# Two FNet and attention layers on one core: three roundings put off, one subtraction moved to VectorE, a bank held longer, the layer norm two steps later

## The chip, the cores and the metric

The kernel runs on one core of a Trainium2 chip. A core has five engines that work side by side, each through its own instructions in the order in which the program issues them: TensorE (PE in the profile; its weight loads are listed apart, as PEld), VectorE (DVE), ScalarE (ACT), GpSimd (POOL) and SyncE (SP, which here only starts DMAs). They wait for each other through semaphores. PE writes its products into PSUM, which has eight banks of 128 x 512 f32; ACT and DVE read PSUM, POOL works only on tiles in SBUF. The metric is the device time of one execution in microseconds, the median of several.

## The reference

Four sublayers work on x (2048 tokens by 512, f32), with a residual sum around each:

```python
x = x + fourier(layernorm(x))
x = x + attention(layernorm(x))
x = x + fourier(layernorm(x))
x = x + attention(layernorm(x))
```

`fourier` is the real part of a DFT over the hidden dimension and over the tokens, given as matrices: with a = x Wd_re and b = x Wd_im it is y = Ws_re a - Ws_im b. `attention` has 32 query heads of 16 and one key and value head shared by all; softmax(q k / 4) v, then the output matrix wo. All of it is f32, so the kernel splits every f32 operand of a product into a high part rounded to the fast product type (fp32r) and a low part, the difference, and multiplies high by high, high by low and low by high (`mm3`).

## The kernel before

The work is split into 16 tiles of 128 tokens (NT) and the sequence DFT into four groups of 512 output tokens (`tb`, 0 to 3). Each of the two layers has a phase A (Fourier, with keys, values and queries of the attention) and a phase B (attention, with the layer norm of the next layer).

**Phase A.** For each group `tb` the sum over the 16 token tiles is made first for the real matrix (c = 0), then for the imaginary one (c = 1). So there are 128 steps n = 32 tb + 16 c + s, with s the token tile. A step multiplies the tile's normalised x (`xnh`, `xnl`) with a piece of the DFT matrix (`ch`, `cl`), into the four banks of tag "x": z[0] to z[3], one for each 128 of the hidden dimension. From n = 48 on (`ROWS`) two steps are done together by `z_rows`, on two halves of PE's rows: in quarters q = 0 to 3 of such a pair the one half of the array works on one bank and the other half on another; banks 0 and 1 are written in quarter 0 and 2, banks 2 and 3 in 1 and 3. After quarters 0 and 1 stands a `relay`, an ACT copy of one column of `xnl` onto itself, which keeps the two halves in order. At the end of a chunk (s = 15) `z_split` copies the banks to SBUF rows on ACT (line 857, "raw"), rounds each to its high part on ACT (line 79) and subtracts for the low part on POOL (line 80). The raw copy is what sets a bank free for the next chunk.

The results of one group are then multiplied with the hidden DFT (`y_tile`, `y_rows`), added to x, and prepared for the attention in the next group's steps (`prep_tasks`, whose work stands in `inner[n, d]`, after quarter-step d of step n): layer norm, four transposes into bank z (`tr_tile`, line 275, with the copies of `split_act` on ACT, lines 83 and 84, and its subtraction on POOL, line 85), keys and values (`kv`, lines 88 to 90), their transposition (`v_tr`, lines 339 and 340, in bank z too) and the queries (`q_mm`).

**Early maxima.** Softmax needs the largest score of each row. Part of these scores is computed already in phase A, in the gaps of DVE and ACT: the table `EARLY` lists groups of score products with a first step and a due step. `pump` is called between PE's products and puts out one product (line 526) if a planner, a Python model of the clocks of PE, DVE and ACT (`clk`, advanced by `spend`), says that a bank is free: the one of tag "z" or one of the three of tag "y". There are three kinds: a whole product whose maximum DVE takes directly (part "u", line 542), a difference product whose positive part ACT writes to SBUF (part "d", line 530, Relu), and a base product that DVE adds to such a part while taking the maximum (part "b", line 536). `flush(n)` forces out what is due at step n. `held` tells the planner until when a bank is taken. All of this is fixed when the program is built; on the chip the engines only follow the order.

**Phase B.** For each of 16 query tiles i there are 32 steps of four score products (line 1086, tag "x"), four exponentials on ACT (line 1088) and the products with v (line 1100); in between the remaining maxima of the next tile (lines 435 and 1046 on PE, 436 and 1051 on DVE, with a one-element DVE copy, 1048, that keeps an order). At step 25 POOL rounds the negated maxima of the next query tile (`max_neg_b`, lines 588 and 589), at step 26 DVE transposes them (`max_rows`, line 594) and DMAs from SP's and POOL's queues put them beside the queries. `out_tasks(i)` lists what becomes of the tile before: its output product, and in the first layer the next layer norm: `o_ln` (line 191 on POOL), `o_xnh` (1250) and `o_xnl` (1254), at steps 25, 26 and 27. In a step the tasks of `out_tasks` are issued ahead of those of `half_tasks` and of `max_neg_b` and `max_rows`. In the last layer the three norm tasks issue nothing.

Of the kernel before, what the change touches and what calls it, by code (L numbers as in the profile page):

```python
# [22 lines left out]
NT = S // P  # L23
# [25 lines left out]
def fnet_mqa_kernel(ctx: ExitStack, tc: tile.TileContext, x_in, ct, dt_, wq, wkv, wo, out):  # L49
    nc = tc.nc  # L50
# [5 lines left out]
    def f(ap):  # L56
        return ap.bitcast(F32)
# [21 lines left out]
        nc.scalar.copy(hi, raw)  # L79
        (eng or nc.vector).tensor_sub(lo, raw, f(hi))  # L80

    def split_act(ps_, hi, lo, raw, neg=False):
        nc.scalar.activation(raw, ps_, AF.Copy, scale=-1.0 if neg else 1.0)
        nc.scalar.copy(hi, raw)
        nc.gpsimd.tensor_sub(lo, raw, f(hi))

    def mm3(ps_, ah, al, bh, bl, start, stop):
        nc.tensor.matmul(ps_, ah, bh, start=start, stop=False)  # L88
# [108 lines left out]
    def make_layer(L, src, mid, dst, last):  # L197
# [69 lines left out]
        def wq_load(g):  # L267
            wq_get(g, [half(2 * (g % 2) + j, F32R) for j in range(2)])

        def tr_tile(t, x, xth, xtl, raw=None):  # L270
            spend(pe=0.6, act=1.2)
            clk["z"] = clk["act"]
            pt = bank("z")
            for k in range(NK):
                nc.tensor.transpose(pt[:, k * P:(k + 1) * P], x[:, k * P:(k + 1) * P], ident)
            v = [ap.rearrange("p (a b) -> p a b", a=NK) for ap in (pt, raw or pt)]
            if raw:
                split_act(v[0], xth, xtl, v[1])
            else:
                split_ps(v[0], xth, xtl)  # L280

# [54 lines left out]
        def v_tr(t0, n, vt):  # L336
            pv_ = bank("z")[:, :n * 32].rearrange("p (t d) -> p t d", t=n)
            for j in range(n):
                nc.tensor.transpose(pv_[:, j, :], vt[32:64, j * P:(j + 1) * P], ident[32:64, 32:64])
            nc.scalar.copy(v1[:, t0:t0 + n, :DH], pv_[:, :, DH:])  # L340

        def q_mm(tb, g, xth, xtl):
            wh, wl = st["wqh", g]
# [157 lines left out]
        def issue(e, pr, g, force):  # L501
            i, kb = EARLY[e][:2]
            tag = "z" if clk["z"] <= clk["y"][0] and not st["hold"] else "y"
            free = clk["z"] if tag == "z" else clk["y"][0]
            part = "u"
            if len(kb) == 2:
                t = turn(e, g)
                if t is None:
                    return False
                part, pr, m = t  # L510
            if part == "b":
                free = max(free, st["rel"][e, pr, g][2] - 0.7)
            if free > clk["pe"] + 0.05 and not force:
                return False
            if tag == "y" and st.get("kept") == 1:
                return False
            if "mxe" not in st:
                st["mxe"] = sb.tile([P, len(KEPT), NPAIR, 2], F32, name="mxe")
            to = st["mxe"][:, KEPT.index(EARLY[e]), pr, g:g + 1] if i else partial(0)[:, pr, g, kb[0]:kb[0] + 1]
            gs = slice(64 * g, 64 * g + KR)  # L520
            k, c0 = (st["kd"], 0) if part == "d" else (kz, 512 * kb[-1])
            pm = bank(tag)
            if tag == "y" and st.get("kept"):
                st["kept"] -= 1
                assert st["kept"]
            nc.tensor.matmul(pm, o.qT[i][gs, pr, :], k[gs, c0:c0 + 512], start=True, stop=True)  # L526
            ready = max(clk["pe"], free) + 0.5
            if part == "d":
                r = sb.tile([P, 512], F32, name=m)
                nc.scalar.activation(r, pm, AF.Relu)  # L530
                end = serve("act", max(ready, clk.get(m, 0.0)))
                st["rel"][e, pr, g] = r, m, end
                seen[e][0][g] += 1
            elif part == "b":
                r, m, done = st["rel"].pop((e, pr, g))
                nc.vector.tensor_tensor_reduce(r, pm, r, 1.0, -3.0e38, ALU.add, ALU.max, to)
                end = clk[m] = serve("dve", max(ready, done))
                seen[e][1][g] += 1
                if i == 0 and (pr, g) == (NPAIR - 1, 1):
                    nc.gpsimd.tensor_copy(partial(0)[:, :, :, kb[1]], partial(0)[:, :, :, kb[0]])  # L540
            else:
                nc.vector.reduce_max(to, pm, axis=AX.X)
                end = serve("dve", ready)
            held(tag, end)
            clk["pe"] += 0.116
            return True
# [188 lines left out]
        def prep_tasks(tb, x1):  # L735
            base = 32 * (tb + 1)
            ts = {}

            def alloc():
                st["xt"] = [slot(2 + j, F32R).rearrange("p (k t) -> p k t", k=NK) for j in range(2)]  # L740

            def tr(tt):
                xth, xtl = st["xt"]
                cs = slice(tt * P, (tt + 1) * P)
                tr_tile(4 * tb + tt, x1[tt], xth[:, :, cs], xtl[:, :, cs], half(4 + tt))

            def do_kv():
                st["vt"] = kv(4 * tb, 4, *st["xt"], now=False)

            def ap(j):  # L750
                return lambda: (spend(dve=0.8), ln_apply(x1[j], x1[j], 4 * tb + j))

            def hold():
                st["hold"] = True

            def tr_(tt):
                st["hold"] = False
                tr(tt)

            def root_(e):  # L760
                roots[e] = ln_root(4 * tb + e, 2)

            ts[0, 0] = [alloc, lambda: root_(0)]
            ts[0, 2] = [lambda: ln_inv(*roots[0])]
            ts[1, 1] = [ap(0), lambda: root_(2)]
            ts[1, 2] = [ap(1), hold]
            ts[1, 3] = [lambda: ln_inv(*roots[2])]
            ts[2, 0] = [vacate, lambda: tr_(0)] + ([k_raw] if tb == 2 else [])
            ts[2, 1] = [hold]
            ts[2, 2] = [ap(2)]  # L770
            ts[2, 3] = [ap(3), lambda: tr_(1)]
            ts[3, 0] = [hold]
            ts[3, 1] = [lambda: tr_(2)]
            ts[3, 2] = [hold]
            ts[4, 0] = [lambda: tr_(3), lambda: [wq_load(g) for g in range(2)]]
            ts[4, 3] = [lambda: keep(2.6)]
            ts[5, 1] = [do_kv]
            ts[6, 0] = [lambda: (kv_lo(4 * tb, 4), k_diff(tb)), hold]
            ts[6, 2] = [lambda: (st.update(hold=False), v_tr(4 * tb, 4, st["vt"]))]
            for g in range(4):  # L780
                ts[6 + g, 1] = [lambda: keep(0.9)]
                ts[6 + g] = [lambda g=g: q_mm(tb, g, *st["xt"])]
                if g < 2:
                    ts[6 + g].append(lambda g=g: wq_load(g + 2))
                if g:
                    ts[6 + g].append(lambda g=g: q_store(tb, g - 1))
            ts[10] = [lambda: q_store(tb, 3)]
            return {(base + k[0], k[1]) if isinstance(k, tuple) else base + k: v for k, v in ts.items()}

        def phase_a(extra):  # L790
# [53 lines left out]
                ks = iter(range(1, 9))  # L844
                return lambda: at.get(next(ks), lambda: None)()

            def z_split(z, hi, lo, c, d, row):
                if d % 2 == 0:
                    return
                if row is None:  # L850
                    for e in (d - 1, d):
                        split_ps(z[e], hi[:, e, :], lo[:, e, :], neg=bool(c))
                    return
                spend(act=2.4)
                raw = [half(row + e) for e in (d - 1, d)]
                for r, e in zip(raw, (d - 1, d)):
                    nc.scalar.activation(r, z[e], AF.Copy, scale=-1.0 if c else 1.0)  # L857
                for r, e in zip(raw, (d - 1, d)):
                    split_sb(r, hi[:, e, :], lo[:, e, :], nc.gpsimd)

            def z_rows(z, odd, chunks, first, last, split):
                turns = [(j, u) for j in range(len(chunks)) for u in range(3)]
# [53 lines left out]
            for n in range(128):  # L916
# [21 lines left out]
                elif n % 2 == 0:  # L938
                    hl = [hls.pop(n + j) for j in range(2)]
                    if n < 112:  # L940
                        rows = z_rows(z, s // 2 % 2, [(s + j, *hl[j]) for j in range(2)], s == 0, s == NT - 2,
                                      lambda d: z_split(z, zh[c], zl[c], c, d, 4))
                    else:
                        h, sp = divmod(n - 112, 8)
                        rows = z_rows(z[4 * h:4 * h + 4], sp // 2 % 2,
# [17 lines left out]
                if n % 32 == 31 and tb < 3:  # L963
# [5 lines left out]
                    for k, v in prep_tasks(tb, dict(x1)).items():  # L969
                        for fn in v:  # L970
                            if isinstance(k, tuple):
                                inner.setdefault(k, []).append(fn)
                            else:
                                add(k, fn)
            assert not inner, inner
            y_tile(3, 2, zh, zl, x1[2])
            qT_load(1)
            o.loaded.add(1)
# [360 lines left out]
            }  # L1339

        def out_tasks(i):
            return {
                1: [lambda: o_store(i, 1), lambda: o_sum(i, 1), lambda: x_load(i)], 5: [lambda: o_inv(i, 1)],
                6: [lambda: o_load(i, 1)], 9: [lambda: o_scale(i, 1)], 10: [lambda: o_hi(i, 1)],
                15: [lambda: o_stats(i, 0)], 16: [lambda: o_stats(i, 1)], 17: [lambda: o_stats(i, 2)],
                18: [lambda: o_stats(i, 3)], 19: [lambda: o_stats(i, 4)],
                20: [lambda: o_rstd(i, 0)], 21: [lambda: o_rstd(i, 1)],
                25: [lambda: o_ln(i)], 26: [lambda: o_xnh(i)], 27: [lambda: o_xnl(i)],
            }

        woh = wol = osp = None
# [48 lines left out]
```

## Time and profile before

| what | value |
|---|---|
| median of three runs | 3493.92 us (3493.11 to 3495.45) |
| the profiled execution | 3492.74 us, span 3491.0 us |
| PE busy | 3453.2 us (99% of the span) |
| ACT busy, DVE busy | 2676.8 us (77%), 2656.2 us (76%) |
| POOL busy | 934.8 us (27%) |
| phase A of the two layers | about 0 to 630 us and 1750 to 2370 us |
| phase B of the two layers | about 630 to 1750 us and 2370 to 3491 us |

Times of rows are microseconds from the span's start. A row of the timeline has the start, the length, engine, line, operation, out<-in, shapes, a count, and in brackets the engine's idle time before it with what ended it. A row of the waits has who waited for whom, the sum, the number and the longest. A row of the windows has the stretch, its length, then for PE, PEld, DVE, ACT and POOL the busy time with the number of instructions, the granted PE clock, the share of the DMA engines and their GB/s. PE's products overlap, so the distance between starts tells its pace better than the lengths do.

### The profile page before, as it was taken

The page shows a single profiled execution, that of the slowest core. Times are in us where ns is not written, and L with a number is a line of the kernel's source. Part 1 is how long each engine was busy: PE and PEld are TensorE (multiplying, and loading weights), DVE is VectorE, ACT ScalarE, POOL GpSimd, SP SyncE. Part 2 cuts the span into 40 slices and gives each one's busy share as a digit, 9 for nine tenths or more (in the row PEclk, how much of TensorE's full clock was granted, in tenths as well). Part 3 has the DMA queues.
Part 4 walks back from the last instruction along what each step waited for, and adds up shares of the span by engine and source line. Part 5 has one row for each costly group of instructions (what it writes and reads, how often), then busy time and mean ns, then how long its engine had stood idle before and what let it go on. Part 6 is the DMA issues. An engine that isn't in the chain of part 4 may idle for free.

```text
span 3491.0 us, 68657 instructions
## 1 busy us (share of the span) xinstructions
PE 3453.2 (99%) x25536; PEld 2017.3 (58%) x25536; DVE 2656.2 (76%) x5768; ACT 2676.8 (77%) x5354; POOL 934.8 (27%) x1476
## 2 busy tenths in 40 slices
PE   8999999999999999999999999999999999999999
PEld 6887979544444444444378979794444444444443
DVE  6264766899999999999432747668989998999892
ACT  4324644899999999999933256549999999999998
POOL 4255443212122222222313353522111111111111
PEclk9999999999999999999999999999999999999999
DMA  6445252321111100111143352423111111011100
GB/s 188 152 149 187 74 167 82 89 61 35 35 35 50 35 26 23 50 35 26 41 139 115 126 168 92 150 78 91 49 38 35 49 37 38 23 36 38 38 23 26
DMA packets 225555, 255.89 MB, mean 73 GB/s; under 512 B 52896, under 2 KB 175040, under 8 KB 218052
## 3 DMA queue, kind: packets, MB, share of 16 engines
q1 hardware_dynamic: 210932, 234.04, 21.9%
q0 software_dynamic: 14144, 17.33, 1.6%
q8 instruction: 201, 3.29, 0.4%
q14 instruction: 134, 1.10, 0.1%
q10 hardware_dynamic: 144, 0.13, 0.0%
HBM read 187.69 MB, written 65.79 MB: 73 GB/s over the span
## 4 chain that ended last, share of the span: by engine, by line
PE 68%; issue 1%; ACT 1%; POOL 1%; DVE 1%; DMA 0%; SPq 0%; DVEq 0%; ACTq 0%; POOLq 0%
PE z L1100 25%; PE x L1086 11%; PE y L1046 8%; PE y L435 7%; PE x L870 5%; PE y L88 2%; PE y L89 2%; PE y L90 2%; PE x L88 1%; PE x L90 1%; PE x L89 1%; PE y L526 1%; PE y L1086 1%; PE z L526 1%; PE x L650 0%
## 5 line engine op out<-in xcount | busy, mean ns | idle before, releaser
L1088 ACT ACTIVATE slot<-x 128x512 f32<-128x512 f32 x3992 | 2053.3, 620 | 31.9 <-PE x L1086 12.2
L436 DVE TENSOR_REDUCE mxp<-y 128x1 f32<-128x512 f32 x1952 | 1259.6, 686 | 62.7 <-PE y L435 7.1
L1100 PE MATMUL z<-slot,v 128*32 128x512 f32 x8192 | 1096.5, 605 | 1.0 <-ACT row L1109 1.0
L1086 PE MATMUL x<-slot,kz 64*128 64x512 f32 x2968 | 836.5, 431 | 0.3 <-DMA slot<-craw 0.2
L1051 DVE TENSOR_REDUCE mxp<-y 128x2 f32<-128x512 f32 x960 | 655.4, 683 | 0.9 <-PE y L1046 0.9
L1046 PEld LDWEIGHTS y<-kz,slot 64*128 64x128 f32 x1408 | 258.6, 184 | 582.3 <-DVE mxp L436 568.5
L435 PE MATMUL y<-kz,slot 64*128 64x512 f32 x1440 | 571.2, 417 | 0.6 <-DVE mxp L436 0.4
L1086 PEld LDWEIGHTS x<-slot,kz 64*128 64x128 f32 x2968 | 438.4, 184 | 81.6 <-issue 41.0
L1046 PE MATMUL y<-kz,slot 64*128 64x256 f32 x1408 | 469.7, 334 | 2.2 <-DVE y L1048 1.8
L870 PE MATMUL x<-cl,xnh 64*128 64x512 f32 (+1 forms) x1536 | 360.2, 355 | 0.0
L870 PE MATMUL x<-ch,xnh 64*128 64x512 f32 (+1 forms) x1536 | 345.1, 359 | 5.1 <-ACT row L857 4.9
L870 PE MATMUL x<-ch,xnl 64*128 64x512 f32 (+1 forms) x1536 | 344.6, 359 | 0.3 <-ACT xnl L637 0.2
L435 PEld LDWEIGHTS y<-kz,slot 64*128 64x128 f32 x1440 | 263.7, 185 | 73.2 <-DVE y L1048 28.1
L1100 PEld LDWEIGHTS z<-slot,v 128*32 128x32 f32 x8192 | 164.3, 108 | 224.6 <-issue 193.3
L1146 POOL TENSOR_TENSOR row<-row,row 128x256 f32<-128x256 f32 x63 | 46.5, 738 | 691.8 <-DMA row<-rd 670.4
L870 PEld LDWEIGHTS x<-ch,xnh 64*128 64x128 f32 x1536 | 211.2, 185 | 25.6 <-ACT row L857 7.4
L870 PEld LDWEIGHTS x<-cl,xnh 64*128 64x128 f32 x1536 | 218.7, 186 | 10.6
L1048 DVE COPY y<-y 1x1 f32<-1x1 f32 x960 | 141.2, 147 | 108.9 <-PE y L1046 102.9
L870 PEld LDWEIGHTS x<-ch,xnl 64*128 64x128 f32 x1536 | 210.8, 186 | 18.8 <-issue 6.4
L79 ACT CAST ch<-craw 128x512 fp32r<-128x512 f32 x176 | 106.6, 626 | 123.1 <-PE x L90 84.5
L526 PE MATMUL y<-kz,slot 64*128 64x512 f32 x496 | 193.3, 397 | 0.4
L88 PE MATMUL x<-ch,xnh 128*128 128x512 f32 x384 | 153.8, 401 | 8.6 <-ACT ch L79 8.6
(230 smaller groups left out, 5455.7 us busy)
## 6 DMA issues: line engine op xcount, KB each, us to landing
craw<-ct_in SPq DMA_DIRECT2D x112, 512.0 KB
slot<-qd SPq DMA_DIRECT2D x44, 1024.0 KB
qd<-row SPq DMA_DIRECT2D x144, 128.0 KB
od<-row SPq DMA_DIRECT2D x252, 64.0 KB
row<-wqd SPq DMA_DIRECT2D x48, 256.0 KB
row<-x_in SPq DMA_DIRECT2D x32, 256.0 KB
mid<-row POOLq DMA_DIRECT2D x32, 256.0 KB, 2.4
craw<-ct_in SPq DMA_DIRECT2D x32, 256.0 KB
```

The source lines that it names most:

```text
L79: nc.scalar.copy(hi, raw)
L88: nc.tensor.matmul(ps_, ah, bh, start=start, stop=False)
L435: nc.tensor.matmul(pm, o.qT[i][gs, pr, :], kz[gs, c0:c0 + n], start=True, stop=True)
L436: nc.vector.reduce_max(to, pm, axis=AX.X)
L526: nc.tensor.matmul(pm, o.qT[i][gs, pr, :], k[gs, c0:c0 + 512], start=True, stop=True)
L870: nc.tensor.matmul(z[d], a[gs, s, d * P:(d + 1) * P], b[gs, :], start=first and q < 2 and e == 0, stop=last and q > 1 and e == len(turns) - 1)
L1046: nc.tensor.matmul(pm[:, 256 * g:256 * g + 256], o.qT[i][gs, pr, :], kz[gs, c0:c0 + 256], start=True, stop=True)
L1048: nc.vector.tensor_copy(pm[:1, 256:257], pm[:1, :1])
L1051: nc.vector.reduce_max(partial(i)[:, pr, :, k], pm.rearrange("p (a n) -> p a n", a=2), axis=AX.X)
L1086: nc.tensor.matmul(e, kz[64 * g:64 * g + KR, c * P:(c + 1) * P], o.qT[i][64 * g:64 * g + KR, cp:cp + 4, :], start=True, stop=True)
L1088: nc.scalar.activation(ptiles[i, s_][:, j, :], e, AF.Exp, scale=DH ** -0.5)
L1100: nc.tensor.matmul(a[32 * j:32 * j + 32, :], v1[:, c, :], pt[:, j, :], start=c == 0, stop=c == NT - 1)
```

## The change

1. `z_split` at the end of a first chunk (c = 0) of the steps done in pairs, that is at n = 79 and n = 111 in each layer, no longer rounds all four rows at once. At the first call (after quarter 2) the second of its two roundings with its subtraction is put into `inner` at step n + 1, quarter-step 2; at the second call (after quarter 3) both go to step n + 2, quarter-steps 0 and 2. Between the two calls `st["calm"]` keeps `issue` from putting out a part "d".
2. The planner is told of ACT's time for a split in smaller pieces: 1.1 for two copies and 0.6 for each rounding, where 2.4 stood ahead of the copies. This holds for all splits through rows.
3. The low part of the last transposed tile of a group (tt = 3) is subtracted by DVE, where POOL did it.
4. After `v_tr` the planner counts bank z as taken for another 1.4.
5. `flush(128)` stands after the last step.
6. The three norm tasks in phase B go to steps 27, 28 and 29 for tiles 0 to 14.
7. `split_act` copies by `scalar.copy` and has lost its unused argument for the sign.

```diff
-    def split_act(ps_, hi, lo, raw, neg=False):
-        nc.scalar.activation(raw, ps_, AF.Copy, scale=-1.0 if neg else 1.0)
+    def split_act(ps_, hi, lo, raw, eng=nc.gpsimd):
+        nc.scalar.copy(raw, ps_)
         nc.scalar.copy(hi, raw)
-        nc.gpsimd.tensor_sub(lo, raw, f(hi))
+        eng.tensor_sub(lo, raw, f(hi))
...
             nc.scalar.copy(v1[:, t0:t0 + n, :DH], pv_[:, :, DH:])
+            held("z", clk["pe"] + 1.4)
...
-            if free > clk["pe"] + 0.05 and not force:
+            if free > clk["pe"] + 0.05 and not force or part == "d" and st.get("calm"):
                 return False
...
-                tr_tile(4 * tb + tt, x1[tt], xth[:, :, cs], xtl[:, :, cs], half(4 + tt))
+                tr_tile(4 * tb + tt, x1[tt], xth[:, :, cs], xtl[:, :, cs], half(4 + tt), nc.vector if tt == 3 else nc.gpsimd)
...
-            def z_split(z, hi, lo, c, d, row):
+            def z_split(z, hi, lo, c, d, row, late=False):
...
-                spend(act=2.4)
                 raw = [half(row + e) for e in (d - 1, d)]
                 for r, e in zip(raw, (d - 1, d)):
                     nc.scalar.activation(r, z[e], AF.Copy, scale=-1.0 if c else 1.0)
-                for r, e in zip(raw, (d - 1, d)):
-                    split_sb(r, hi[:, e, :], lo[:, e, :], nc.gpsimd)
+                cut = [lambda r=r, e=e: (spend(act=0.6), split_sb(r, hi[:, e, :], lo[:, e, :], nc.gpsimd))
+                       for r, e in zip(raw, (d - 1, d))]
+                spend(act=1.1)
+                at = []
+                if late:
+                    at = [(0, 2)] if d == 1 else [(1, 0), (1, 2)]
+                    st["calm"] = d == 1
+                for fn in cut[:len(cut) - len(at)]:
+                    fn()
+                for (j, k), fn in zip(at, cut[len(cut) - len(at):]):
+                    inner.setdefault((int(st["n"]) + 1 + j, k), []).append(fn)
...
-                                      lambda d: z_split(z, zh[c], zl[c], c, d, 4))
+                                      lambda d: z_split(z, zh[c], zl[c], c, d, 4, not c))
...
             assert not inner, inner
+            flush(128)
...
+            late = 2 if i < NT - 1 else 0
...
-                25: [lambda: o_ln(i)], 26: [lambda: o_xnh(i)], 27: [lambda: o_xnl(i)],
+                25 + late: [lambda: o_ln(i)], 26 + late: [lambda: o_xnh(i)], 27 + late: [lambda: o_xnl(i)],
```

More of the change, by code (lines that the diff above doesn't have):

```diff
@@ L268, in wq_load, with tr_tile @@
             wq_get(g, [half(2 * (g % 2) + j, F32R) for j in range(2)])
-        def tr_tile(t, x, xth, xtl, raw=None):
+        def tr_tile(t, x, xth, xtl, raw=None, eng=nc.gpsimd):
             spend(pe=0.6, act=1.2)
@@ L277, in tr_tile @@
             if raw:
-                split_act(v[0], xth, xtl, v[1])
+                split_act(v[0], xth, xtl, v[1], eng)
             else:
```

## The prediction

> **What bounds the kernel now.** I read the page first, then the waits of PE and DVE, then windows for the granted clock, then the timeline at each place where PE stood.
>
> ```profile
> PE 3453.2 (99%) x25536; PEld 2017.3 (58%) x25536; DVE 2656.2 (76%) x5768; ACT 2676.8 (77%) x5354; POOL 934.8 (27%) x1476
> ```
>
> PE never rests for long, so nothing but its own stalls can be won. The waits name them:
>
> ```profile
> PE x L870 <- ACT row L857: 4.9, 4, 1.3
> PE y L89 <- POOL slot L85: 4.9, 2, 3.0
> PE z L526 <- ACT v L340: 2.0, 2, 1.0
> ...
> DVE mt L594 <- POOL ms L589: 14.0, 4, 5.0
> ```
>
> The first three are waits in phase A, each the same in both layers: for the raw copies of a finished chunk, for the low part of a transposed tile before keys and values, and for bank z after the transposed values. The fourth is in phase B, of DVE, and PE hangs on DVE there. The sums look small (12 us on PE), but a stall also has a tail: the granted clock halves behind some of them.
>
> ```profile
> 289.00:295.80 6.80, 5.96 (x15) 4.29 (x17) 0.00 (x0) 0.83 (x2) 1.74 (x3) 0.50 0.39 116
> 2026.40:2029.80 3.40, 3.40 (x9) 2.61 (x9) 0.00 (x0) 0.00 (x0) 0.00 (x0) 0.50 0.32 123
> 2258.50:2261.90 3.40, 3.40 (x33) 3.40 (x31) 2.01 (x6) 2.55 (x7) 3.40 (x4) 0.50 0.02 5
> 521.70:525.10 3.40, 3.27 (x39) 2.76 (x41) 1.79 (x5) 3.19 (x8) 2.44 (x3) 1.00 0.00 0
> 899.97:903.39 3.42, 3.42 (x20) 1.55 (x16) 2.28 (x5) 1.18 (x3) 3.42 (x8) 0.50 0.06 6
> ```
>
> The last column but two is the clock. It is 0.50 in four of these stretches, 17.0 us in all. The stall of the first layer at 521.7 has no such tail, the same one of the second layer (2257) has.
>
> **The change, part by part.**
>
> **Low part by VectorE.** First group with early work (tb = 1), both layers, and for the normal pace the same twelve products in group tb = 2:
>
> ```profile
> 283.44 0.62 ACT L84 CAST slot<-row 128x512 fp32r<-128x512 f32 x1
> ...
> 286.39 0.50 PE L88 MATMUL y<-slot,wkvh 128*128 128x512 f32 x1
> ...
> 288.53 1.26 POOL L85 TENSOR_TENSOR slot<-row,slot 128x512 fp32r<-128x512 f32 x1
> ...
> 294.83 0.79 PE L870 MATMUL x<-ch,xnl 64*128 64x512 f32 x2
> ...
> 296.08 0.39 PE L870 MATMUL x<-ch,xnl 64*128 64x512 f32 x2
> ```
>
> ```profile
> 459.22 0.50 PE L88 MATMUL y<-slot,wkvh 128*128 128x512 f32 x1
> ...
> 462.24 0.50 PE L870 MATMUL x<-ch,xnl 64*128 64x512 f32 x2
> ```
>
> ```profile
> 2023.73 0.50 PE L88 MATMUL y<-slot,wkvh 128*128 128x512 f32 x1
> ...
> 2030.44 0.51 PE L870 MATMUL x<-ch,xnl 64*128 64x512 f32 x2
> ```
>
> The normal block takes 462.24 - 459.22 = 3.02. In the second layer it took 2030.44 - 2023.73 = 6.71: 3.7 lost. In the first layer 294.83 - 286.39 = 8.44, 5.4 lost; the three groups that follow take 1.25 to 296.08 where three times 0.23 is 0.69, so 6.0 lost. The high part is there at 284.06, but POOL subtracts at 288.53, behind two roundings for the next steps. DVE has nothing in this stretch (its column is 0.00 at 289 to 295.8). Its price is in this row, minimum, median, maximum:
>
> ```profile
> L80 DVE TENSOR_TENSOR slot<-row,slot x16: 679/686/1789, 66.3 to 1817.3; 128x512 fp32r<-128x512 f32 x16
> ```
>
> At 0.69 the low part is ready at 284.8, at 1.79 at 285.9; PE asks for it at 286.6. Gain 6.0 + 3.7 = 9.7.
>
> The Trainium skill (SBUF — State Buffer, "Who interferes with whom") says that a VectorE instruction with two SBUF inputs and a GpSimd one that reads SBUF keep each other out until the first is done. This speaks against the move, since POOL subtracts until 284.7 here; the maximum of 1789 ns in the row agrees with it. By that rule the low part comes at 285.4, still in time, so the sum is the same by both.
>
> In group tb = 2 DVE isn't idle:
>
> ```profile
> 455.30 0.62 ACT L84 CAST slot<-row 128x512 fp32r<-128x512 f32 x1
> 455.32 1.89 DVE L542 TENSOR_REDUCE mxe<-y 128x1 f32<-128x512 f32 x3 [0.66 <-PE y L526]
> ```
>
> The subtraction is issued ahead of these maxima and waits for the rounding until 455.92, then takes 0.69: the maxima start at 456.6, 1.3 late, with PE's next early products behind them, which need the banks. The planner counts no DVE time for it. Bounds: 0 (free banks cover it) to 1.3 + 1.1 (the row's maximum less its median) = 2.4 a layer. I take 1.1, as only three banks stand between: 2.2 for both layers. Group tb = 0 has no early work, nothing there.
>
> **Roundings put off, no part "d" between.** The end of the chunk at n = 79, and below it at n = 111:
>
> ```profile
> 347.21 1.16 ACT L79 CAST slot<-row 128x512 fp32r<-128x512 f32 x2
> ...
> 348.73 0.47 PE L870 MATMUL x<-ch,xnl 64*128 64x512 f32 x2
> ...
> 349.21 0.64 ACT L530 ACTIVATE qraw<-y 128x512 f32<-128x512 f32 x1
> 349.69 1.14 ACT L857 ACTIVATE row<-x 128x512 f32<-128x512 f32 x2
> ...
> 350.39 0.98 PE L870 MATMUL x<-ch,xnh 64*128 64x512 f32 x2 [1.19 <-ACT row L857]
> ...
> 351.44 0.40 PE L870 MATMUL x<-ch,xnl 64*128 64x512 f32 x2
> ```
>
> ```profile
> 520.16 0.28 PE L870 MATMUL x<-ch,xnl 64*128 64x256 f32 x1
> ...
> 522.42 0.39 PE L870 MATMUL x<-ch,xnl 64*128 64x256 f32 x2
> ```
>
> From 348.73 to 351.44 PE does three groups, 0.69 at pace, and one early product (0.12): 1.9 lost. From 520.16 to 522.42 three groups of half the width, 0.35: 1.9 lost. ACT's order is two raw copies, two roundings, three Relu parts (the last at 349.21), and only then the two raw copies that PE waits for, at 349.69. One rounding and three Relus are taken from between; ACT starts a piece about every 0.48 (349.21 to 349.69), so the copies come 4 x 0.48 = 1.9 earlier, at 347.8. That is the whole stall. Four places: 7.6. In the second layer the half clock behind n = 111 goes too: between 0.5 (33 instructions against 39 in the like stretch) and 1.7 (half of 3.40); 1.1.
>
> What is put off comes back. The three roundings go where the planner sees ACT free again, but the held-back Relus may all come in the first quarter of the next chunk, ahead of its relay. Two to three of them there make the relay 0 to 0.6 late: 0.3 at each of four places, 1.2. On POOL the six subtractions stay the same six, with those for the next steps ahead; no DMA of these steps moves. For all other splits the planner now counts 2.3 (1.1 + 2 x 0.6) where it counted 2.4: early products shift by 0.1, nothing.
>
> **Bank z held longer.**
>
> ```profile
> 467.60 0.49 PE L870 MATMUL x<-ch,xnh 64*128 64x512 f32 x2
> ...
> 469.10 0.50 PE L526 MATMUL z<-kz,slot 64*128 64x512 f32 x1 [1.00 <-ACT v L340]
> ```
>
> An early product was sent into z while the values still stood in it: 1.50 where 0.23 is due, 1.27 lost, in each layer 2.5. With 1.4 more on the planner's clock the product goes to a "y" bank or comes 1.4 later, when ACT is done.
>
> **Layer norm two steps later.**
>
> ```profile
> 896.45 2.07 POOL L191 TENSOR_SCALAR row<-row,mv,rs 128x512 f32<-128x512 f32 x1
> ```
>
> ```profile
> 899.06 0.24 DVE L594 STREAM_TRANSPOSE mt<-ms 128x64 f32<-128x64 f32 x1 [2.10 <-POOL ms L589]
> ```
>
> ```profile
> 972.65 0.24 DVE L594 STREAM_TRANSPOSE mt<-ms 128x64 f32<-128x64 f32 x1 [2.10 <-POOL ms L589]
> ```
>
> The norm takes 2.07 of POOL ahead of the rounding of the maxima, and DVE waits just that long, in two tiles; without it POOL is ready when DVE is. The first loses 2.1 and half of the 3.42 us at half clock, at most 3.8, and PE was busy all that time, so 3.5; the second 2.1. Together 5.6. The other two waits of line 594 (4.8 and 5.0 by the sum of 14.0) stand at steps where no norm task is. At steps 27 to 29 the norm now stands ahead of the next tile's scaling and rounding on POOL, which nobody needs before step 13 of the next tile; POOL's own DMAs of step 26, which carry the maxima, now go ahead of the norm's rounding and not behind it. I cost the new place at nothing: POOL is 27% busy by the page, and xnh is first read in the next phase A.
>
> **flush(128)** costs what the planner has left over. Early work now ends about 2 us before the last step (rows below); the change holds it back by about as much. None to three products a layer; 0.5 each layer, 1.0. `scalar.copy` for the Copy activation: ACT's copies and casts of this size take 0.60 to 0.62 in all rows; 0.
>
> **Sum:** 9.7 + 7.6 + 1.1 + 2.5 + 5.6 = 26.5; less 2.2, 1.2 and 1.0: 22.1. The profiled execution took 3492.74 (span 3491.0), so 3470.6; the median of the runs is 1.2 above it: **3471.8**. With every cost at its lower bound it is 3467, with the upper ones (4.8, 2.4, 4.1) 3479.
>
> **The rivals.**
>
> *The half clock stays.* Of the 26.5, the tails are about 3.0, 1.7, 1.1 and 1.7 = 7.5. For it: the clock did not fall at 521.7 and fell at 2257 behind the same stall, so something other than the stall decides too; smaller stalls that stay could bring it. Against it: the two longest stalls, of keys and values, both have the tail, and no stall as long is left. It gives 3479. The Trainium skill (TensorE: Matmul & The Clock Gate, "Part 1: The HAM clock gate") has the clock fall after an idle window of about 3.4 us that runs freely, whatever the kernel does. The rows agree in the length (3.40, twice that at 289) but not in the cause: an idle stretch of 3.0 (line 85) and shorter ones sufficed.
>
> *The waits change places.* Relus and roundings crowd the next chunk's start, relay and raw copies wait as before, and DVE's subtraction costs its bound: 7.6 less, less 2.6 more: 3471.8 + 10.2 = 3482. For it: ACT's work is only moved, and it stands in one queue. Against it: ACT is idle most of the next quarters.
>
> *It does not do what it says.* Both together, 3489.5: no difference that a measurement of this kernel can tell (0.2%, 7 us).
>
> *Slower.* The early work no longer fits, and `flush` forces it out at the due steps, PE waiting for a DVE piece of 0.69 with each product:
>
> ```profile
> 596.28 0.39 PE L526 MATMUL y<-kz,slot 64*128 64x512 f32 x1
> ```
>
> ```profile
> 598.43 0.28 PE L870 MATMUL x<-ch,xnh 64*128 64x256 f32 x1
> ```
>
> There are 2.15 us to spare, three products. To eat 22 and be 7 slower it takes 29 / (2 x 0.69) = 21 left over in each layer, 16.6 us of delay (2.15 + 21 x 0.69); the change holds back for 1.4 at each of two chunk ends and 1.4 after the values. It would give 3501 or more.
>
> **How the numbers follow.** Forecast 0.58, its own range 3465 to 3477; half clock stays 0.14; waits change places 0.14; no difference 0.09; slower 0.05. The first three are faster by more than 0.2%: 0.86. The range goes from 3464 (all terms without a cost, and some noise) to 3486, past the third case.
>
> **What would show it.** Right: keys and values of tb = 1 take about 3.0 in both layers; no wait of PE for line 857 or 340 over 0.3; no DVE wait of 2.10 for line 589; clock 1.00 at those places. Wrong: reduces of tb = 2 about 1.3 later with PE behind them by more than 2; relays late by over 1 at n = 80 and 112; early products in a row after the last line 870 product; new stretches at half clock.

## The result

The changed kernel took 3471.34 us (median of six runs, 3469.57 to 3473.84), the kernel before 3494.16 us beside it (3492.79 to 3497.70). The ratio is 0.9935, 95% interval 0.9924 to 0.9946: 22.8 us faster. The profiled execution took 3471.86 us, its span is 3469.8 us, 21.2 less than before. New code shifts the line numbers: the groups are now at 879 (870 before), the early products at 527 (526), their maxima at 543 and 537 (542, 536), the Relu at 531 (530), the relay at 638 (637), the maxima's transposition at 595 (594). The raw copies stay at 857.

The page of the kernel after, the line of its engines:

```profile
PE 3441.7 (99%) x25536; PEld 2011.9 (58%) x25536; DVE 2659.1 (77%) x5774; ACT 2676.3 (77%) x5354; POOL 928.8 (27%) x1470
```

PE does the same number of products. Six subtractions went from POOL (1476 to 1470) to DVE (5768 to 5774). PE is busy 11.5 us less, in part because less of its work ran at half clock; the rest of the 21.2 is standstill that went. Its waits after (who waited for whom, sum, number, longest):

```profile
PE x L879 <- ACT xnl L638: 2.8, 4, 0.8
PE y L527 <- DVE mxe L543: 2.2, 2, 1.2
PE y L527 <- DVE mxp L537: 1.3, 2, 0.7
```

The waits for the raw copies (4.9 before), the low part (4.9) and bank z (2.0) are not among the twelve longest any more. Three others are: four for the relay, two for the maxima that the subtraction now stands ahead of (line 543), and two for maxima of line 537, one in each layer at n = 122, which are taken up below. Gone too are the two waits of before by which PE hung on DVE in phase B (waits of the kernel before):

```profile
PE y L1046 <- DVE y L1048: 3.7, 2, 1.8
```

The waits of DVE for line 590 (589 before) go from 14.0 in four to 9.9 in two:

```profile
DVE mt L595 <- POOL ms L590: 9.9, 2, 5.0
```

**Keys and values of tb = 1** (timeline after, first layer, then second):

```profile
280.97 3.83 POOL L85 TENSOR_TENSOR slot<-row,slot 128x512 fp32r<-128x512 f32 x3
...
284.13 1.77 DVE L85 TENSOR_TENSOR slot<-row,slot 128x512 fp32r<-128x512 f32 x1 [6.89 <-ACT slot L84]
...
286.44 0.50 PE L88 MATMUL y<-slot,wkvh 128*128 128x512 f32 x1
...
289.43 0.50 PE L879 MATMUL x<-ch,xnl 64*128 64x512 f32 x2
```

```profile
2007.49 0.69 DVE L85 TENSOR_TENSOR slot<-row,slot 128x512 fp32r<-128x512 f32 x1 [6.04 <-ACT slot L84]
...
2009.79 0.50 PE L88 MATMUL y<-slot,wkvh 128*128 128x512 f32 x1
...
2012.78 0.50 PE L879 MATMUL x<-ch,xnl 64*128 64x512 f32 x2
```

Both blocks take 2.99 now (8.44 and 6.71 before). In the first layer the subtraction took 1.77, for POOL was still at its own three until 284.80; it was done at 285.90, well ahead of the product of line 89 that reads it, which starts at about 286.8.

**The end of the chunk at n = 79** (timeline after):

```profile
341.72 1.12 ACT L857 ACTIVATE row<-x 128x512 f32<-128x512 f32 x2
342.68 1.18 ACT L79 CAST ch<-craw 128x512 fp32r<-128x512 f32 x2
343.71 0.65 ACT L531 ACTIVATE rel<-y 128x512 f32<-128x512 f32 x1
344.20 0.64 ACT L531 ACTIVATE kraw<-y 128x512 f32<-128x512 f32 x1
...
344.29 0.42 PE L879 MATMUL x<-ch,xnl 64*128 64x512 f32 x2
...
344.68 0.65 ACT L531 ACTIVATE qraw<-y 128x512 f32<-128x512 f32 x1
345.15 0.26 ACT L638 CAST xnl<-xnl 128x2 fp32r<-128x2 f32 x1
...
345.47 0.51 PE L879 MATMUL x<-ch,xnl 64*128 64x512 f32 x2 [0.76 <-ACT xnl L638]
```

The raw copies come in time. But all three Relus that were held back between the two calls now stand ahead of the next chunk's relay, and PE stands from 344.29 to 345.47 where 0.23 is due: 0.95 lost.

**Group tb = 2** (timeline after):

```profile
448.36 1.03 DVE L85 TENSOR_TENSOR slot<-row,slot 128x512 fp32r<-128x512 f32 x1 [1.28 <-ACT slot L84]
...
449.31 1.87 DVE L543 TENSOR_REDUCE mxe<-y 128x1 f32<-128x512 f32 x3
450.05 0.49 PE L527 MATMUL y<-kz,slot 64*128 64x512 f32 x1 [1.18 <-DVE mxe L543]
```

DVE stands 1.28 until ACT's rounding is there and then subtracts for 1.03; PE waits 1.18 for the bank whose maximum is behind that.

**The tile in phase B** where DVE had waited 2.10 (timeline after):

```profile
888.29 0.21 POOL L589 CAST ms<-nm 128x32 fp32r<-128x32 f32 x1
888.58 0.25 POOL L590 TENSOR_TENSOR ms<-nm,ms 128x32 fp32r<-128x32 f32 x1
...
888.88 0.23 DVE L595 STREAM_TRANSPOSE mt<-ms 128x64 f32<-128x64 f32 x1
889.67 3.92 POOL L601 DMA_DIRECT2D xnl<-mt  x8 [0.84 <-PE y L1056]
893.63 2.08 POOL L191 TENSOR_SCALAR row<-row,mv,rs 128x512 f32<-128x512 f32 x1
```

The transposition follows the subtraction at once, and the norm comes 5 us later, behind the DMAs.

**The ledger.** It compares the times of the same PE products in both traces. The gain of a stretch is how much closer its first and last group stand (early products that moved over a border counted at 0.1155 each). Negative is gained:

```
stretch                                      layer 1   layer 2   predicted (both)
n = 68 to 70, keys and values of tb = 1       -5.89     -3.73     -9.7
n = 80 to 82, behind the chunk of n = 79      -1.02     -1.02  \  -7.5 (7.6 and 1.1
n = 112 to 116, behind the one of n = 111     -1.31     -2.37  /  less 1.2)
n = 100 to 102, VectorE's share of tb = 2     +1.51     +1.32     +2.2
n = 102 to 104, bank z                        -1.35     -1.36     -2.5
n = 94 to 98                                  -0.54     -0.51      0
n = 118 to the end                            +0.79     +0.37     +1.0
phase B, two tiles of layer 1                 -5.76               -5.6
```

With small rests it is 13.6 us in the first layer and 7.5 in the second. The +1.0 forecast for the last stretch was meant for `flush(128)`.

### The profile page after: what moved, and what is told of

The parts are those of the page before. It is cut to its first block, busy times and chain, and to the rows that moved or that the text cites. A ratio compares the mean times of both kernels' runs of the same rounds, so it can differ in the third digit from the quotient of the medians.

```text
span 3469.8 us, 68639 instructions
## 1 busy us (share of the span) xinstructions
PE 3441.7 (99%) x25536; PEld 2011.9 (58%) x25536; DVE 2659.1 (77%) x5774; ACT 2676.3 (77%) x5354; POOL 928.8 (27%) x1470
## 4 chain that ended last, share of the span: by engine, by line
PE 91%; issue 3%; ACT 2%; POOL 2%; DVE 1%; DMA 1%; SPq 0%; DVEq 0%; ACTq 0%; POOLq 0%
PE z L1110 29%; PE x L1096 13%; PE x L879 11%; PE y L1056 10%; PE y L436 8%; PE y L88 3%; PE y L527 3%; PE y L89 2%; PE y L90 2%; PE x L90 2%; PE x L88 2%; PE x L89 2%; PE z L527 1%; PE y L1096 1%; PE z L275 1%
## 5 line engine op out<-in xcount | busy, mean ns | idle before, releaser
L879 PEld LDWEIGHTS x<-ch,xnl 64*128 64x128 f32 x1536 | 212.6, 184 | 21.2 <-issue 6.1
```

The lines of the kernel that those rows point to most:

```text
L879: nc.tensor.matmul(z[d], a[gs, s, d * P:(d + 1) * P], b[gs, :], start=first and q < 2 and e == 0, stop=last and q > 1 and e == len(turns) - 1)
```

## The experiments

All were timed beside the kernel before. `low_pool` to `z_free` ran on one chip (before: 3491.77 us), `same_again` to `both` on a second (3492.98), the last four on a third (3493.17). Ratios have intervals of about 0.0012 to each side, so single steps of 2 to 4 us are read from the traces, and the times only bear them out. A "tail" below is what a stall costs beyond its own length, PE working at half clock behind it.

**Undo the low part by VectorE.**

```diff
-tr_tile(..., half(4 + tt), nc.vector if tt == 3 else nc.gpsimd)
+tr_tile(..., half(4 + tt))
```

> The changed kernel, with the low part of the last transposed tile on POOL again. My theory: the stall of keys and values in group tb = 1 comes back with its half clock (5.9 us in the first layer, 3.7 in the second by the two traces) and the wait of the maxima in tb = 2 goes (1.5 and 1.3): 6.8 us slower than the changed kernel, about 3478. Rival, the half clock belongs to free windows and not to the stall: only the standing itself returns (about 3.2 and 2.2), less 2.8: about 3474.

Measured: 3473.42 us, ratio 0.9949 (0.9936 to 0.9961); the profiled span is 3474.5, 4.7 over the changed kernel's. By the ledger n = 68 to 70 lose 5.9 and 3.6 again, n = 100 to 102 win back 1.6 and 1.4. But the profiled execution is the slowest of the five (3476.26) and has half clock behind both stalls. By the medians the run is 3.1 to 4.9 above the changed kernel (ratios 0.9940 and 0.9935), short of the 6.8 expected and nearer to the rival's 2.6 without tails; why tails differ from execution to execution is worked out further down. The wait of before is back in the waits of this kernel:

```profile
PE y L89 <- POOL slot L85: 4.8, 2, 2.9
```

**Undo the later norm.**

```diff
-late = 2 if i < NT - 1 else 0
+late = 0
```

> The changed kernel, with the three norm tasks at steps 25 to 27 again. My theory: the two DVE waits of 2.10 us for the rounded maxima return at query tiles 3 and 4 of the first layer and cost 3.6 and 2.1: about 3477. Rival without a tail of half clock: 2 x 2.1, about 3475.5. If the order on POOL was not what held DVE, nothing changes: 3471.

Measured: 3473.80 us, 0.9952 (0.9940 to 0.9965), span 3472.0. By the ledger 4.1 come back, all in phase B of layer 1, and the waits of DVE are four again:

```profile
DVE mt L595 <- POOL ms L590: 14.2, 4, 5.1
```

In this execution no half clock followed either wait; in the one of before, one of the two had it. The bare waits are 4.2 of the 5.8, the rest is the tail. By the ratios the run is 4.2 to 5.9 above the changed kernel, which does not choose between the expected 5.7 and the rival's 4.2.

**Undo the roundings put off.**

```diff
-lambda d: z_split(z, zh[c], zl[c], c, d, 4, not c))
+lambda d: z_split(z, zh[c], zl[c], c, d, 4))
```

> The changed kernel, with all four roundings at once again and nothing held back between (the planner's smaller pieces stay). My theory: what the two traces show at the chunk ends comes back, 1.0 and 1.3 us in the first layer, 1.0 and 2.4 in the second (with a half clock): 5.7 slower, about 3477, and 3476 without the half clock. Rival, the waits only changed places and the gain came from elsewhere: within 1 us of 3471.

Measured: 3477.14 us, 0.9959 (0.9945 to 0.9973), span 3475.1: by the median the dearest of the four to undo, though the intervals overlap. The waits of PE for line 857 are back to the tenth:

```profile
PE x L879 <- ACT row L857: 4.9, 4, 1.3
```

Yet only 0.8 to 1.0 come back at three of the four places and 2.1 at the last, which had half clock behind it (from 2242.58 for 3.41): the stall is the old one, the gain had been made smaller by the relay.

**Undo the longer hold of bank z.**

```diff
-            held("z", clk["pe"] + 1.4)
```

> The changed kernel, without the 1.4 for which the planner counts bank z as taken behind the transposed values. My theory: PE waits again for the ACT copy in group tb = 2 of both layers, 1.35 us each: 2.7 slower, about 3474. Rival: the planner, which sees other times from then on, shifts the early products anyway, and the wait falls elsewhere or nowhere: within 1 us of 3471.

Measured: 3472.57 us, 0.9946 (0.9934 to 0.9959), span 3470.6. `PE z` waits for line 340 twice again, 2.0 in all; 2.9 come back in the first layer (with 3.4 us at half clock behind it) and 1.4 in the second. By the ratios the run is 2.1 to 3.8 above the changed kernel; 2.7 were expected.

**The changed kernel again**, on the second chip, as a base for the next three.

> The changed kernel as it is, to stand on the same chip as the three beside it. About 22.5 us below the kernel before. By my theory its runs differ by their half clock alone: the spread goes with the granted clock, about 1.7 us for each 0.0005 of it.

Measured: 3470.88 us (3469.30 to 3471.73), 0.9940 (0.9928 to 0.9953): 22.1 below before. Of its five runs the fastest has the mean clock 1.000 and the other four 0.999, too coarse to test the 1.7 us for each 0.0005.

**Hold the Relus until the relay.** Part "d" stays held back after the second call too, until the first relay of the next chunk is issued:

```diff
-                    st["calm"] = d == 1
+                    st["calm"] = True
...
                     if q < 2:
+                        if first:
+                            st["calm"] = False
                         relay(...)
```

> The changed kernel, with parts d held back until the next chunk's first relay is out, and not only until the second call of the split. My theory: the two relays that the three Relus make late (0.95 us at n = 80 and 0.7 at n = 112, in each layer) come in time: 3.3 us faster than the changed kernel. Rival: the Relus are then late for what follows, at the second relay or at the due steps, and the wait moves there: within 1 us of the changed kernel.

Measured: 3467.38 us (3465.57 to 3467.91), 0.9930 (0.9917 to 0.9942): 3.5 below the changed kernel on the same chip, with no run of the one among those of the other. The relay now stands ahead of the Relus (timeline of this kernel):

```profile
341.85 1.12 ACT L857 ACTIVATE row<-x 128x512 f32<-128x512 f32 x2
342.82 1.18 ACT L79 CAST ch<-craw 128x512 fp32r<-128x512 f32 x2
343.85 0.25 ACT L638 CAST xnl<-xnl 128x2 fp32r<-128x2 f32 x1
343.94 0.65 ACT L531 ACTIVATE rel<-y 128x512 f32<-128x512 f32 x1
```

The ledger gives 0.95, 0.9, 0.95 and 0.9 at the four places, 3.7 in all, and nothing is lost later. So the late relay was what part 1 had left over.

**VectorE's low part in tb = 0 and 1 alone.**

```diff
-nc.vector if tt == 3 else nc.gpsimd
+nc.vector if tt == 3 and tb < 2 else nc.gpsimd
```

> The changed kernel, with VectorE's subtraction in groups tb = 0 and 1 only and POOL's in tb = 2. My theory: the maxima of tb = 2 no longer wait behind it, 1.5 us in the first layer and 1.3 in the second: 2.8 faster. Rival: POOL's low part is now late for keys and values there, which begin 0.1 us after it was ready in the trace of before: within 1 us of the changed kernel, or slower by the half clock's tail.

Measured: 3467.38 us (3465.20 to 3467.54), 0.9929 (0.9916 to 0.9941), 3.5 below the changed kernel. n = 100 to 102 win 1.4 in each layer; the wait for line 543 is gone from the list. In tb = 2 POOL's low part ends at 451.83 and keys and values, begun at 451.43, don't wait for it.

**Both together.**

> The two edits of the kernels beside it together. They touch different places, so by my theory they add up: 6.1 us faster than the changed kernel, a ratio of about 0.992 to the kernel before. Rival: the later early products of the one reach the group tb = 2 of the other, and less than 4 of it is left.

Measured: 3463.29 us (3461.73 to 3464.18), 0.9918 (0.9905 to 0.9932), 7.6 below the changed kernel on the same chip: 3.5 and 3.5 add up. It beats both kernels. Of the longest waits of PE in phase A the late relay and the maxima of line 543 are gone, those of line 537 at n = 122 stay (waits of this kernel):

```profile
PE x L88 <- ACT ch L79: 8.4, 1, 8.4
PE x L90 <- POOL xnl L717: 2.0, 4, 0.9
PE y L527 <- DVE mxp L537: 1.3, 2, 0.7
```

**Part 3 alone**, put into the kernel before:

```diff
+        eng.tensor_sub(lo, raw, f(hi))      # split_act, with its copy by scalar.copy
...
+tr_tile(..., half(4 + tt), nc.vector if tt == 3 else nc.gpsimd)
```

> The kernel before with part 3 alone (and the copy by scalar.copy): the low part of the last transposed tile by VectorE, nothing else. PE's order is that of before. My theory, by the ledger of the two traces: keys and values of tb = 1 gain 5.9 and 3.7, the maxima of tb = 2 lose 1.5 and 1.3, so 6.8 below before, ratio 0.9981. Rival A: the profiled execution of before had more of the half clock behind these stalls than most executions have; then only the bare stalls count, 3.0 twice less 1.2 twice, 3.6 below before, ratio 0.9990. Rival B: the time gained is lost at the next wait: within 1 us of before.

Measured: 3487.34 us, 0.9983 (0.9974 to 0.9991), 5.8 below before. The ledger gives 5.9 and 3.7 gained, 1.3 and 1.3 lost, and 6.7 less span. The interval holds the expected 0.9981 and barely rival A's 0.9990; rival B is out. By the median, what the profile showed of the tails is nearly what the runs have.

**Roundings put off, Relus not held back.**

```diff
-                    st["calm"] = d == 1
+                    st["calm"] = False
```

> The changed kernel with the roundings put off, but without holding back part d between the two calls of the split. In its order of instructions three early products of part d stand ahead of the last groups of the chunk at n = 79. If the Relus ahead of the raw copies are what costs, the raw copies of the second call come 3 x 0.48 = 1.4 later again, while the relay of the next chunk is no longer 0.9 late: 0.5 at each of four places, 2 us above the changed kernel, ratio about 0.9944. Rival A: the roundings alone were in the way; then the raw copies come in time and the relay too, 3.5 below the changed kernel, 0.9928. Rival B: holding back does all and the rounding nothing: all of the 4 to 5 us come back that undoing the whole part cost, 0.9950.

Measured: 3469.85 us, 0.9932 (0.9919 to 0.9946). The interval excludes rival B (0.9950) and holds both the expected 0.9944 and rival A's 0.9928, so the time alone does not choose. The trace has the expected delay of the raw copies, but not its price. The timeline of this kernel:

```profile
341.29 0.64 ACT L79 CAST slot<-row 128x512 fp32r<-128x512 f32 x1
341.80 0.63 ACT L531 ACTIVATE rel<-y 128x512 f32<-128x512 f32 x1
342.29 0.63 ACT L531 ACTIVATE kraw<-y 128x512 f32<-128x512 f32 x1
342.77 0.64 ACT L531 ACTIVATE qraw<-y 128x512 f32<-128x512 f32 x1
343.24 1.14 ACT L857 ACTIVATE row<-x 128x512 f32<-128x512 f32 x2
...
343.95 0.98 PE L879 MATMUL x<-ch,xnh 64*128 64x512 f32 x2 [0.43 <-ACT row L857]
```

The three Relus stand ahead of the raw copies and make them 1.5 later, as was expected; PE waits for them, and the relay is in time. By the ledger the two kernels lose the same within 0.25 at both chunk ends of both layers. So at the chunk ends the hold of the change, from the first call to the second, is worth nothing by itself: the Relus cost the same ahead of the raw copies as ahead of the relay.

The two profiled spans still differ, by 1.8 us (3468.0 here), and by the ledger that lies at the end of phase A: from n = 118 on this kernel is 1.0 shorter in the first layer and 0.7 in the second. There the changed kernel's PE stands for the maxima of line 537 (timeline of the changed kernel, n = 122):

```profile
566.01 0.49 PE L527 MATMUL y<-kd,slot 64*128 64x512 f32 x1 [0.67 <-DVE mxp L537]
```

The second layer has the same wait at 2288.30, this kernel has neither. So with the hold the planner puts the early products in an order that costs PE time in the last steps. That this is a price of any hold is not shown: without the hold and with the roundings at once (`no_late`) PE waits there too, 0.87 at 567.95. The times alone do not hold the two kernels apart.

**A stall made on purpose.** To see what a stall drags behind it, VectorE makes the subtraction of tb = 1 three or five times over, in the version with both edits:

```diff
-        eng.tensor_sub(lo, raw, f(hi))
+        for _ in range(3 if eng is nc.vector else 1):      # the other run: 5
+            eng.tensor_sub(lo, raw, f(hi))
...
-nc.vector if tt == 3 and tb < 2 else nc.gpsimd
+nc.vector if tt == 3 and tb == 1 else nc.gpsimd
```

> The best version so far (the three Relus held back until the first relay, VectorE's low part in group tb = 1 alone), in which VectorE makes the same subtraction three times in tb = 1. The single one ends at 285.8, PE asks at 286.6; two more of 0.7 to 1.0 each end at 287.2 to 287.8, so PE stands still for 0.6 to 1.2 in each layer. If a stall is worth its own length, 1.2 to 2.4 us above that version (0.9918), ratio 0.9922 to 0.9925. Rival: any stall over 1 us brings 3.4 us at half clock behind it, which costs up to 1.7 more in each layer: up to 5.8, ratio up to 0.9935, and clock 0.50 for 3.4 us in the windows behind 287.

> As the run with three subtractions, with five: they end at 288.6 to 289.8, PE stands still for 2.0 to 3.2 in each layer, the length of the stall in the kernel before. If a stall is worth its own length, 4 to 6.4 us above the best version, ratio 0.9930 to 0.9937. If a stall of this length has a tail at half clock as in the profile of before (in the first layer 3.0 of stall and 3.0 behind it, in the second 3.0 and 0.7), 7.7 to 10 us above it, ratio 0.9940 to 0.9947, and clock 0.50 behind 289 and behind 2020 in the windows.

Measured: three times 3468.67 us, 0.9929 (0.9916 to 0.9941), five times 3474.63 us, 0.9948 (0.9935 to 0.9960); by the ratios 3.8 and 10.5 above the version with both. Both intervals still reach the most that was expected of bare stalls (0.9925 and 0.9937), so what follows is read from the traces. The subtractions took longer than I expected (three took 4.48 in the first layer, beside POOL's work), so the stalls were 1.82 and 0.76 us with three, 4.00 and 3.20 with five. By the ledger they cost 3.6 and 1.0 with three, 5.6 and 3.5 with five. So the stall of 1.82 has a tail of 1.8 and the one of 4.00 of 1.6, but the one of 3.20 has next to none (0.3). The length of the stall alone does not decide.

What does decide is seen in the traces' times at which the granted clock changes. In the kernel before it falls at 288.99, 899.97, 2026.37, 2258.48 and 2367.70. The distances are 179, 330, 68 and 32 times 3.4133 us, each to within 0.01, and so it is in every trace here, with another offset in each. So the clock is judged on a grid that runs by itself. Here are windows cut on that grid; the columns are the stretch, its length, the busy time of PE, PEld, DVE, ACT and POOL with the instructions, the granted clock, the DMA share, GB/s. First the kernel before, behind n = 111 in the first and in the second layer, and keys and values of tb = 1 in both:

```profile
517.68:521.09 3.41, 2.76 (x36) 2.33 (x32) 1.09 (x4) 3.41 (x9) 1.84 (x2) 1.00 0.01 2
521.09:524.51 3.42, 2.68 (x30) 2.17 (x32) 1.20 (x3) 3.42 (x9) 2.46 (x3) 1.00 0.00 0
2255.07:2258.48 3.41, 2.01 (x25) 1.61 (x25) 0.00 (x0) 3.41 (x8) 2.45 (x3) 1.00 0.01 2
2022.96:2026.37 3.41, 1.50 (x10) 0.78 (x7) 0.00 (x0) 0.00 (x0) 3.03 (x3) 1.00 0.19 35
285.57:288.98 3.41, 1.32 (x9) 0.57 (x5) 0.00 (x0) 0.00 (x0) 3.33 (x4) 1.00 0.33 127
```

Then the run with five subtractions, first and second layer, the first layer of the run with three, and the kernel before with part 3 alone, behind n = 111 in the first layer:

```profile
287.57:290.98 3.41, 0.00 (x0) 0.00 (x0) 3.34 (x3) 0.00 (x0) 3.33 (x4) 1.00 0.00 0
...
2011.30:2014.71 3.41, 1.81 (x13) 0.95 (x11) 3.34 (x3) 0.20 (x1) 3.33 (x3) 1.00 0.29 105
2014.71:2018.12 3.41, 1.81 (x8) 1.52 (x9) 1.42 (x2) 0.00 (x0) 0.17 (x1) 1.00 0.45 154
```

```profile
286.33:289.74 3.41, 1.59 (x9) 0.92 (x6) 2.40 (x2) 0.00 (x0) 3.33 (x3) 1.00 0.17 63
289.74:293.16 3.42, 3.42 (x10) 2.19 (x9) 0.00 (x0) 0.00 (x0) 1.13 (x3) 0.50 0.64 223
```

```profile
515.36:518.77 3.41, 2.00 (x27) 1.60 (x26) 0.00 (x0) 3.41 (x8) 2.52 (x2) 1.00 0.00 0
```

At keys and values the clock fell behind each window with PE busy 1.59 or less (and one with 1.67, from 2013.14 in `low_pool`) and behind neither of those with 1.81. The stall of 3.20 is cut in two halves by the border at 2014.71, and neither half is enough. Behind n = 111 the same stall was cut at 521.09 in the first layer (2.76 and 2.68 busy, no fall) and lay in one window in the second (2.01, fall): that is why the one had a tail and the other not. `low_dve_only` bears it out: there the stall of the first layer lies in one window (the last line, 2.00), the clock falls behind it at 518.77, and by the ledger 1.1 more is lost than in the execution of before. The border between falling and not isn't one number for all work: windows of phase B with 2.01 (`norm_back`, from 887.46) and 2.07 (before, from 971.66) kept the clock; in phase A one with 2.22 kept it (before, from 347.02) and one with 2.30 lost it (`z_free`, from 459.92); and between the phases, at about 620 and 2345, some with 2.4 to 3.0 lost it. What exactly is counted is open.

## Why the prediction was right, point by point

The forecast, 3471.8 us, stands 0.5 from the median. Its sum of 22.1 compares with 21.2 between the two profiled executions and 22.8 between the medians; some of its terms were off, and they cancelled in part. That the forecast came within 0.5 is therefore partly luck; the direction and the four parts are not.

- **Low part by VectorE, 9.7:** 9.62 by the ledger; undone it comes back, and alone it gives 9.6 as well. Of the 1.1 between 0.69 and 1.79 at which the subtraction could end, it took nearly all: 1.77, while POOL subtracted until 284.80. The Trainium skill (SBUF — State Buffer, "Who interferes with whom") had it this way, a two-input VectorE instruction kept waiting by a GpSimd one that reads SBUF. The row agrees, but it ends at 285.90, 0.5 later than the 285.4 worked out by that rule; POOL had gone on to a rounding (284.75 to 285.35), and what took the rest isn't shown. There was time enough either way, as PE reads the low part at 286.8.
- **Its cost in tb = 2, 2.2:** 2.8, in the bounds of 0 to 4.8. DVE stood 1.28 for the rounding, as was said, but subtracted for 1.03 and not 0.69.
- **Roundings put off, 7.6, tail 1.1, relay late 1.2:** net 7.5 forecast, 5.7 measured. The step that failed is "Two to three of them there make the relay 0 to 0.6 late: 0.3". All three Relus came into the first quarter at once and made it 0.95 late at n = 80. `calm_longer` shows it: with the Relus behind the relay 3.7 more are won by the ledger, 3.5 by the times. So the term put at 1.2 for the four places was worth 3.7. At those chunk ends the rival "the waits change places" was half true, and `no_calm` shows how exactly: held or not, the same three Relus cost the same.
- **Bank z, 2.5:** 2.7. Undone, 1.4 in the layer without a tail.
- **Norm two steps later, 5.6:** 5.76; 4.1 of it came back when undone, in an execution without a tail there. The new place costs nothing that the ledger shows.
- **flush(128), 1.0:** the last early product starts at 588.16 and at 2310.52, 2.7 ahead of the last product of line 879 in each layer, so none was left over and the term is 0 as it was meant. The rival "slower" had no ground here. Yet 1.2 were lost from n = 118 on (0.8 and 0.4), as much as the term. At n = 122 PE stands 0.67 in each layer for maxima of line 537, a wait that the sum doesn't have. That the sizes agree is luck.
- **The half clock.** Here the term was right for a reason I didn't have. The tails were put at 7.5 of 26.5 (7.2 by the terms as they stand in the sum, where the norm's 3.5 holds 1.4 of tail and not 1.7). The mean granted clock of the runs bears out the size: 0.996 to 0.998 in most runs of before, 0.998 to 1.000 in those of after, a difference of about 0.002 of 3490 us, 7 us. In the profile after, one stretch is left inside the kernel, 3.41 us from 2346.62. What I called "something other than the stall" is the border of the grid. The Trainium skill (TensorE: Matmul & The Clock Gate, "Part 1: The HAM clock gate") has the clock fall after an idle window of about 3.4 us that runs freely. The grid of 3.4133 us agrees with the length and with the free running. The window doesn't need to be idle, though: the clock fell also behind one with 1.59 us busy of 3.41 (`stall_3`).
- **Not foreseen:** 0.5 gained in each layer at n = 94 to 98, which is left open, and the 0.8 and 0.4 lost from n = 118 on, which `no_calm` gives back.

The sign was never near: by the ledger the four parts won 9.6, 5.7, 2.7 and 5.8, each shown by its own undoing, and the subtraction's cost in tb = 2 took 2.8.

## What to carry to other kernels

An instruction held back in an in-order queue is not gone: find which wait it meets next and hold it past that one too (here the relay, 3.5 us). Moving work to an idle engine pays only at the steps where that engine is idle; decide it per step and not per kind (the same edit won 9.6 at tb = 1 and lost 2.8 at tb = 2). Count a stall of TensorE of about 1 us or more (in `z_free` one of 0.99 had a tail) with a tail that may or may not come, since its place against a grid that shifts from run to run has a say; a single profile gives one draw.

## What the runs showed of the hardware

- The granted TensorE clock changes on a grid of 3.4133 us, whose offset differs from execution to execution. A stall of 1.82 us inside one window cost 3.6 (`stall_3`), one of 3.20 cut in halves by a border cost 3.5, one of 4.00 cost 5.6 (both `stall_5`).
- Three VectorE subtractions in a row beside POOL's work took 4.48 us in the first layer and 3.42 in the second (`stall_3`), where a single one took 0.69 in the second layer of the changed kernel; a rounding of POOL beside them took 1.08 and 1.07, where the one before it took 0.64 and 0.60.
